# Value loads of a head in one shared 72-KB place, in 48-KB rows, and another order in the last head

## The chip, the cores and the metric

The kernel runs on one core of one Trainium2 chip. The metric is device time in microseconds (us) of one execution.

## The reference, cut to what matters

One token of a decoder layer: layer norm, attention over a long cache, a projection with residual, then a small two-layer network with residual.

```python
B, Sq, D = 1, 1, 640
H, Sk, Dh = 32, 32768, 192
q = (layernorm(x) @ wq).reshape(B, Sq, H, Dh).transpose(0, 2, 1, 3)
p = softmax(einsum("bhqd,bhkd->bhqk", q, k_cache) * Dh ** -0.5)
o = einsum("bhqk,bhkd->bhqd", p, v_cache)
h = x + o.transpose(0, 2, 1, 3).reshape(B, Sq, H * Dh) @ wo
out = h + relu(layernorm(h) @ w1) @ w2          # Dff = 1536
```

All inputs are bfloat16. The two caches hold 32 heads x 32768 rows x 192 numbers x 2 bytes each, 805 MB together; the weights bring the traffic to 825 MB. All of it is read once.

## The kernel before

A head's 32768 keys are handled in 8 chunks. In a chunk each of the 128 partitions has 32 rows. Of these DVE scores 12 or 16 (a multiply and a reduction) and PE the rest (transposes into PSUM, copies by ACT into SBUF, matmuls with the query). ACT takes the exponentials, and PE then multiplies them with the value rows, "the sums" below (`values`). SyncE issues all loads from one queue and waits, before each, until the place it writes is free; what is issued and not yet taken by the 16 DMA engines is what the texts call "the rings". GpSimd passes on the landing of a load to PE and DVE ("relay"; in the lines such a wait ends with `<-POOLq`).

```python
kt = [sbuf(f"kt{i}", [P, JK * Dh], bf16, 512) for i in range(NK)]   # 2 x 48 KB per partition
va = sbuf("va", [P, JK * Dh], bf16, 512)                            # 48 KB
vb = sbuf("vb", [P, JL * Dh], bf16, 512)                            # 24 KB

def vals(h, ld):
    if ld == 1:
        g.wait("PV", h, 1)                   # sums of chunk 1 of this head are done
    elif h > 0:
        g.wait("PV", h - 1, 3 if ld == 0 else NC - 1)
    src = rows(v_hd, h, P * JK * (ld // 2), JK)
    if ld < 2:
        src = src[:, ld * JL * Dh:(ld + 1) * JL * Dh]               # half a 48-KB row
    load((vb, vb, va)[ld][:], src, "dva" if ld == 2 else "dvb", "v", h, ld)
...
for h in range(LAST):
    keys(h, 0)
    vals(h, 0)
    keys(h, 1)
    for ld in ((2, 1) if h == 0 else (1, 2)):
        vals(h, ld)
```

So a head has five loads: keys 6.3 MB, values 3.1 MB, keys 6.3 MB, values 3.1 MB, values 6.3 MB. The last head is written by hand: its keys come in six loads, the last three small, then its values. PE's order there is (cut):

```python
def pe_end(g):
    ...
    transposes(g, h, 5);  scores_pe(g, h, 4)
    transposes(g, h, 6);  scores_pe(g, h, 5)
    transposes(g, h, 7);  scores_pe(g, h, 6)
    transposes(g, h, 8);  scores_pe(g, h, 7)
    transposes(g, h, 9)
    values(g, h, 2);      scores_pe(g, h, 8)
    values(g, h, 3);      scores_pe(g, h, 9)
    for c in (4, 5, 6, 7): values(g, h, c)
    values(g, h, 9); values(g, h, 8, 0); den_mm(g, h); values(g, h, 8, 1)
    ...                     # normalise, project, layer norm, the two layers with w1 and w2
```

The softmax here doesn't subtract the row's maximum and nothing guards it: scores larger than these inputs give would overflow.

Of the kernel before, what the change touches and what calls it, by code (L numbers as in the profile page):

```python
# [80 lines left out]
def kernel(  # L81
# [38 lines left out]

    full = [(c // 4, (c % 4) * J, J, JPS[c % 2]) + ((c // 2, (c % 2) * J) if c < 4 else (2, (c - 4) * J)) for c in range(NC)]

# [7 lines left out]
    def chunks(h):  # L130
        return ends if h == LAST else full

    NBM = max(JPS) * Dh // (2 * P)
# [17 lines left out]
    def sbuf(name, shape, dtype, align=32):  # L151
        return ctx.enter_context(nc.sbuf_tensor(name, shape, dtype, align_bytes=align))
# [5 lines left out]
    kt = [sbuf(f"kt{i}", [P, JK * Dh], bf16, 512) for i in range(NK)]  # L158
    va = sbuf("va", [P, JK * Dh], bf16, 512)
    vb = sbuf("vb", [P, JL * Dh], bf16, 512)  # L160
    wo_s = sbuf("wo_s", [P, 3, D], bf16, 512)
# [28 lines left out]
    for tag in ("ln1", "ln2"):  # L190
# [10 lines left out]

    wq_c = [kt[1][:, c * H * Dh:(c + 1) * H * Dh] for c in range(DT - 1)] + [va[:, 0:H * Dh]]
    assert (DT - 1) * H * Dh == JK * Dh and H * Dh <= JL * Dh

    k_at = {0: kt[0][:, 0:64 * Dh], 1: kt[0][:, 64 * Dh:128 * Dh], 2: kt[1][:, 0:64 * Dh],
            3: kt[1][:, 64 * Dh:104 * Dh], 4: kt[1][:, 104 * Dh:120 * Dh], 5: kt[1][:, 120 * Dh:128 * Dh]}
    v_at = {0: vb[:], 1: va[:, 0:JL * Dh], 2: va[:, JL * Dh:2 * JL * Dh],
            3: vb[:, 0:40 * Dh], 4: vb[:, 40 * Dh:56 * Dh], 5: vb[:, 56 * Dh:64 * Dh]}
    w1_s = kt[0][:, 0:DT * Dff].rearrange("p (c n) -> p c n", n=Dff)
# [7 lines left out]
    def v_tile(h, ld):  # L217
        return v_at[ld] if h == LAST else (vb, vb, va)[ld][:]

# [10 lines left out]
    def dma_program(g):  # L230
# [6 lines left out]
        def keys(h, ld):  # L237
            if h > 0:
                if ld == 0:
                    g.wait("PV", h - 1, 4 if h == 1 else 2)  # L240
                else:
                    g.wait("PV", h - 1, 5)
                g.wait("scs", h - 1, 4 * ld + 3)
            elif ld == 1:
                g.wait("att0")
            load(kt[ld][:], rows(k_hd, h, P * JK * ld, JK), f"dk{ld}", "k", h, ld)

        def vals(h, ld):

            if ld == 1:  # L250
                g.wait("PV", h, 1)
            elif h > 0:
                g.wait("PV", h - 1, 3 if ld == 0 else NC - 1)
            src = rows(v_hd, h, P * JK * (ld // 2), JK)
            if ld < 2:
                src = src[:, ld * JL * Dh:(ld + 1) * JL * Dh]
            load((vb, vb, va)[ld][:], src, "dva" if ld == 2 else "dvb", "v", h, ld)

        for c in range(DT):
            load(wq_c[c], wq_view[:, c * H * Dh:(c + 1) * H * Dh], f"dwq{c}", "wq", c)  # L260
        for h in range(LAST):
            keys(h, 0)
            vals(h, 0)
            keys(h, 1)
            for ld in ((2, 1) if h == 0 else (1, 2)):
                vals(h, ld)
            if h % 2 == 0 and h < LAST - 1:
                if h > 0:
                    g.wait("prj", h)
                load(wo_s[:], wo_view[h // 2], "dwo", "wo", h // 2)  # L270

        def end_keys(i, k0, jl, sem):
            load(k_at[i], rows(k_hd, LAST, k0, jl), sem, "k", LAST, i)
# [4 lines left out]

        g.wait("PV", LAST - 1, 2)
        g.wait("scs", LAST - 1, 3)  # L280
        end_keys(0, 0, JL, "dk0")
        g.wait("PV", LAST - 1, 3)
        end_values(0, 0, JL * Dh, "dvb", "v", LAST, 0)
        end_keys(1, P * JL, JL, "dke0")
        g.wait("PV", LAST - 1, 5)
        g.wait("scs", LAST - 1, NC - 1)
        end_keys(2, 2 * P * JL, JL, "dk1")
        k0 = P * JL * (NL - 1)
        at = []
# [4 lines left out]
        g.wait("PV", LAST - 1, NC - 1)  # L294
        end_values(1, 0, JL * Dh, "dva", "v", LAST, 1)

        for i in range(2):
# [17 lines left out]
    def pool_program(g):  # L315
        e = nc.gpsimd
        g.do(lambda: e.memset(wide[:], 0.0), "pool_act", ("ident0",))
        g.wait("ident0")
        g.do(lambda: e.affine_select(out=wide[:], in_=wide[:], compare_op=A.not_equal, fill=1.0, base=HE,
                                     pattern=[[-1, HE + P + 2 * (P - HE)]], channel_multiplier=1), "pool_row", ("ident",))  # L320
        def key(h, ld):
            relay(g, "k", h, ld)
            g.do(lambda: nc.gpsimd.sem_inc(sems["pool_dve"], 1))  # L323
            book_relay(g, "k", h, ld, sem="pool_dve")

        for h in range(LAST):
            key(h, 0)
            relay(g, "v", h, 0)
            key(h, 1)
            for ld in ((2, 1) if h == 0 else (1, 2)):  # L330
                relay(g, "v", h, ld)
            relay(g, "W", h)
        key(LAST, 0)
        relay(g, "v", LAST, 0)
        key(LAST, 1)
        key(LAST, 2)
        relay(g, "v", LAST, 1)
# [26 lines left out]
    def transposes(g, h, c):  # L364
        ld, off, jc, jp = chunks(h)[c][:4]
        src = k_tile(h, ld)
        if h == LAST and ld >= NL - 1:
            if c == 6 or ld >= NL:
                g.wait("k", h, ld)
        elif off == 0:  # L370
            g.wait("at", "k", h, ld)
# [43 lines left out]
    def values(g, h, c, part=None):  # L415
# [4 lines left out]
        if h == LAST and ld >= NL - 1:  # L420
            g.wait("vc", h, c)
        elif h == LAST and ld == 2:
            g.wait("vh", c - 4)
        elif off == 0:
            g.wait("at", "v", h, ld)
# [73 lines left out]

    SUMS = ((), (), (0,), (1,), (), (), (2, 3), (4,), (5, 6, 7))  # L500
    SUMS_0 = ((), (), (0,), (1,), (), (), (4,), (5,), (2, 3, 6, 7))

    def pe_head(g, h, turn=None):
        for c in range(NC + 1):
            if c == 0 and h > 0:
                den_mm(g, h - 1)
            if c < NC and c != 4:
                transposes(g, h, c)
            for d in (SUMS if h > 0 else SUMS_0)[c]:
                if c < NC:  # L510
                    values(g, h, d)
            if c > 0:
                scores_pe(g, h, c - 1)
            if c == 4:
                transposes(g, h, 4)
            if c == 2 and h > 0:
                o_turn(g, h - 1)
            if c == 4 and h > 0:
                project(g, h)
            if c == 6:  # L520
                q_spread(g, h + 1, turn)
        for d in (SUMS if h > 0 else SUMS_0)[NC]:
            values(g, h, d)

# [18 lines left out]
    def pe_end(g):  # L543
# [14 lines left out]
        transposes(g, h, 5)  # L558
        scores_pe(g, h, 4)
        transposes(g, h, 6)  # L560
        scores_pe(g, h, 5)
        transposes(g, h, 7)
# [3 lines left out]
        transposes(g, h, 9)  # L566
        values(g, h, 2)
        scores_pe(g, h, 8)
        values(g, h, 3)
        scores_pe(g, h, 9)  # L570
        values(g, h, 4)
        for c in (5, 6, 7):
# [72 lines left out]
    def act_head(g, h):  # L645
# [13 lines left out]

        behind = ((0,), (1,), (), (2,), (), (), (3,), (), (4,), ())  # L660
        for c in range(NCM):
# [7 lines left out]
        exp_pe(g, h, NCM - 1)  # L669
        for c in range(5, NCM):  # L670
            exp_dve(g, h, c)
# [242 lines left out]
```

## Time and profile before

| | kernel before |
|---|---|
| time, median | 1917.69 us (1916.72 to 1918.34, 3 runs) |
| span of the profiled run | 1915.3 us |
| last byte of the loads | 1911.3 us |
| end of the last sums on PE | 1904.5 us |
| DMA share and rate, 500 to 1500 us | 1.00, 433 to 434 GB/s |

The page's lines and the windows are shown in the prediction. The last byte and the end of the sums are read from the trace's records of DMA packets and matmuls. Two chains run into the end: the loads, whose last piece is w2, and PE, whose sums must be done before the projection and the two layers can follow. The end is the later of the two.

### The profile page before, as it was taken

To read this page: it belongs to the slowest core of one execution; us is meant where nothing else is said; L and a number is where in the kernel's file an instruction comes from. 1 tells how busy PE (TensorE), PEld (TensorE's weight loads), DVE (VectorE), ACT (ScalarE), POOL (GpSimd) and SP (SyncE) were. 2 spreads that over 40 slices of the span, in tenths; PEclk is the share of its full clock that TensorE was granted. 3 is DMA by queue.
4 is the path that set the end of the run, shared out by engine and by line. 5 is a ranking of instruction groups with operands and counts; after the bars stand their busy time and mean duration, and the time that the engine had idled before them with its cause. 6 is when DMAs were issued, how large, how long until landed. Compare 5 with 4: busy or idle time off the path is not lost.

```text
span 1915.3 us, 36109 instructions
## 1 busy us (share of the span) xinstructions
PE 1554.4 (81%) x15899; PEld 1089.8 (57%) x15899; DVE 1561.4 (82%) x731; ACT 939.4 (49%) x2000; POOL 1.0 (0%) x6
## 2 busy tenths in 40 slices
PE   7777787787888788878879887788788787878888
PEld 7455555554555555555556555556565555555565
DVE  2798787987878978789787888878798787987897
ACT  2455454554544544545545445545355454554454
POOL 0000000000000000000000000000000000000000
PEclk9888998888988889888898888898888898888988
DMA  9999999999999999999999999999999999999998
GB/s 409 428 436 428 430 438 430 437 435 431 436 431 432 435 433 429 437 430 437 435 431 433 434 434 434 432 429 437 430 436 434 430 437 431 435 430 437 431 433 369
DMA packets 29651, 825.29 MB, mean 431 GB/s; under 512 B 3132, under 2 KB 4669, under 8 KB 8125
## 3 DMA queue, kind: packets, MB, share of 16 engines
q1 hardware_dynamic: 29616, 824.98, 99.9%
q8 instruction: 15, 0.25, 0.0%
q14 instruction: 8, 0.06, 0.0%
q10 hardware_dynamic: 12, 0.00, 0.0%
HBM read 824.97 MB, written 0.00 MB: 431 GB/s over the span
## 4 chain that ended last, share of the span: by engine, by line
DVE 39%; DMA 39%; PE 15%; ACT 5%; issue 1%; DVEq 0%; SPq 0%; POOLq 0%
DMA kt<-in_A_k_cache_dram 35%; DVE sc L708 19%; DVE pr L705 18%; PE tp L381 7%; PE o_ps L362 7%; ACT kT L608 5%; DMA va<-in_A_v_cache_dram 2%; PE sp L362 1%; DVE o_pair L720 1%; DMA kt<-in_B_w_dram 1%; ACT pA L623 1%; DVE oT L730 0%; DMA kt<-in_A_wq_dram 0%; DVE rec L713 0%; DVE rec L714 0%
## 5 line engine op out<-in xcount | busy, mean ns | idle before, releaser
L705 DVE TENSOR_TENSOR pr<-kt,qb 128x2304 f32<-128x2304 bf16 (+2 forms) x257 | 756.7, 2944 | 313.8 <-POOLq L323 284.8
L608 ACT COPY kT<-tp 128x1024 bf16<-128x1024 bf16 (+1 forms) x898 | 814.3, 1017 | 271.4 <-PE tp L381 271.4
L381 PE MATMUL tp<-ident_f,kt 128*128 128x128 f32 x3456 | 592.0, 332 | 241.0 <-POOLq L344 165.2
L708 DVE TENSOR_REDUCE sc<-pr 128x12 f32<-128x2304 f32 (+2 forms) x257 | 756.1, 2942 | 8.9
L381 PEld LDWEIGHTS tp<-ident_f,kt 128*128 128x128 f32 x3456 | 487.0, 171 | 291.5 <-POOLq L344 170.9
L362 PE MATMUL o_ps<-va,pB 128*2 128x384 bf16 x1152 | 220.8, 340 | 59.8 <-POOLq L344 59.8
L362 PEld LDWEIGHTS sp<-qm,kT 128*128 128x128 bf16 x6912 | 197.6, 98 | 83.6 <-issue 42.8
L362 PE MATMUL sp<-qm,kT 128*128 128x2 bf16 x6912 | 214.6, 164 | 26.0 <-ACT pB L614 24.5
L362 PE MATMUL o_ps<-vb,pB 128*2 128x384 bf16 x1152 | 214.6, 332 | 22.6 <-ACT pA L623 22.0
L623 ACT ACTIVATE pA<-sc 128x12 bf16<-128x12 f32 (+2 forms) x257 | 58.3, 227 | 349.0 <-DVEq L65 349.0
L614 ACT ACTIVATE pB<-sp 128x20 bf16<-128x20 f32 (+2 forms) x258 | 52.4, 203 | 307.9 <-PE sp L362 307.9
L362 PEld LDWEIGHTS o_ps<-va,pB 128*2 128x2 bf16 x1152 | 94.1, 86 | 155.6 <-POOLq L344 67.5
L362 PE MATMUL o_ps<-va,pA 128*2 128x384 bf16 x896 | 171.5, 333 | 0.0
L362 PE MATMUL o_ps<-vb,pA 128*2 128x384 bf16 x896 | 166.7, 326 | 0.0
L362 PEld LDWEIGHTS o_ps<-vb,pB 128*2 128x2 bf16 x1152 | 90.3, 85 | 123.2 <-ACT pA L623 27.6
L362 PEld LDWEIGHTS o_ps<-va,pA 128*2 128x2 bf16 x896 | 77.0, 86 | 75.3 <-issue 8.3
L362 PEld LDWEIGHTS o_ps<-vb,pA 128*2 128x2 bf16 x896 | 75.2, 84 | 70.2
L614 ACT ACTIVATION_READ_ACCUMULATOR pB<-sp 128x1 f32 x258 | 55.1, 214 | 0.0
L623 ACT ACTIVATION_READ_ACCUMULATOR pA<-sc 128x1 f32 x257 | 53.1, 207 | 0.0
L362 PE MATMUL o_ps<-xn_ln,kt 128*96 128x1 bf16 (+1 forms) x316 | 22.3, 208 | 2.7 <-DMA kt<-in_A_wq_dram 2.7
L362 PEld LDWEIGHTS o_ps<-xn_ln,kt 128*96 128x96 bf16 (+1 forms) x316 | 22.1, 174 | 2.9 <-issue 2.8
L720 DVE TENSOR_SCALAR o_pair<-o_ps,rec 2x384 bf16<-2x384 f32 x32 | 19.3, 604 | 1.5 <-PE o_ps L362 0.4
(69 smaller groups left out, 187.3 us busy)
## 6 DMA issues: line engine op xcount, KB each, us to landing
kt<-in_A_k_cache_dram SPq DMA_DIRECT2D x62, 6144.0 KB, 26.7
vb<-in_A_v_cache_dram SPq DMA_DIRECT2D x63, 3072.0 KB, 19.0
va<-in_A_v_cache_dram SPq DMA_DIRECT2D x31, 6144.0 KB, 26.8
kt<-in_A_k_cache_dram SPq DMA_DIRECT2D x3, 3072.0 KB, 22.1
wo_s<-in_A_wo_dram SPq DMA_DIRECT2D x16, 480.0 KB, 19.0
kt<-in_A_wq_dram SPq DMA_DIRECT2D x4, 1536.0 KB, 10.9
va<-in_A_v_cache_dram SPq DMA_DIRECT2D x1, 3072.0 KB, 31.6
va<-in_A_v_cache_dram SPq DMA_DIRECT2D x2, 1536.0 KB, 36.4
```

The costliest lines, as they stand in the source:

```text
L362: return lambda: pe.matmul(o, lhsT=w, rhs=r, **kw)
L381: calls.append(lambda b=b, o=o: pe.transpose(out=dst[:, b, :], in_=src[:, o:o + 2 * P].bitcast(f32), identity=ident_f[:]))
L608: g.do(lambda: act.copy(out=kT[c % 2][:, b0:b0 + nb, :], in_=src[:, 0:nb, :].bitcast(bf16)), "act_pe", ("cp", h, c, k))
L614: g.do(lambda: act.activation(out=pB[c % NB][:, 0:jp], in_=sp[:, 0:jp], func=F.Exp, scale=SCALE, accum_out=dsums[:, 2 * c + 1:2 * c + 2]), ...
L623: g.do(lambda: act.activation(out=pA[c % NB][:, 0:jd], in_=sc[c % NC][:, 0:jd], func=F.Exp, scale=SCALE, accum_out=dsums[:, 2 * c:2 * c + ...
L705: g.chain(lambda: dve.tensor_tensor(out=pr[:, 0:j1 - j0, :], in0=src[:, (off + j0) * Dh:(off + j1) * Dh].rearrange("p (j d) -> p j d", d=D ...
L708: g.chain(lambda: dve.reduce_sum(out=sc[c % NC][:, j0:j1], in_=pr[:, 0:j1 - j0, :], axis=X), "dve")
L720: g.do(lambda: dve.tensor_scalar_mul(out=o_pair[:, :, 1, :], in0=o_ps[0:2, 0:2 * Dh].rearrange("q (i d) -> q i d", i=2), scalar1=rec[0:2, ...
```

## The change

Its intent: the values of a head come in two loads of 48-KB rows instead of three loads, two of which have 24-KB rows. The two share one 72-KB place: the first lies in thirds 0 and 1, the second in thirds 1 and 2. The chunks in the shared third are summed first. In the last head the second values are loaded ahead of the last keys, and PE and ACT take another order. The diff, cut to its core:

```diff
+    OFFS = (2, 3, 0, 1, 0, 1, 2, 3)
+    full = [(c // 4, OFFS[c] * J, J, JPS[c % 2], c // 4, OFFS[c] * J) for c in range(NC)]
...
-    va = sbuf("va", [P, JK * Dh], bf16, 512)
-    vb = sbuf("vb", [P, JL * Dh], bf16, 512)
+    va = sbuf("va", [P, (JK + JL) * Dh], bf16, 512)
...
         def vals(h, ld):
             if ld == 1:
                 g.wait("PV", h, 1)
             elif h > 0:
-                g.wait("PV", h - 1, 3 if ld == 0 else NC - 1)
+                g.wait("PV", h - 1, 5)
             ...                              # the old source and load go
+            load(v_tile(h, ld), rows(v_hd, h, P * JK * ld, JK), ("dva", "dvb")[ld], "v", h, ld)
...                                           # last head, loads
         end_keys(2, 2 * P * JL, JL, "dk1")
+        g.wait("PV", LAST - 1, 5)
+        end_values(1, 0, JL * Dh, "dvb", "v", LAST, 1)
         ...                                  # the three small key loads
         g.wait("PV", LAST - 1, NC - 1)
-        end_values(1, 0, JL * Dh, "dva", "v", LAST, 1)
...                                           # last head, PE
         scores_pe(g, h, 4)
+        scores_pe(g, h, 5)
+        values(g, h, 2)
+        values(g, h, 3)
         transposes(g, h, 6)
-        scores_pe(g, h, 5)
         transposes(g, h, 7)
         scores_pe(g, h, 6)
         transposes(g, h, 8)
         scores_pe(g, h, 7)
         transposes(g, h, 9)
-        values(g, h, 2)
         scores_pe(g, h, 8)
-        values(g, h, 3)
+        values(g, h, 4)
         scores_pe(g, h, 9)
-        values(g, h, 4)
```

In the loop, PE now takes the transposes and scores of four chunks and then their sums, in step with the loads.

More of the change, by code (lines that the diff above doesn't have):

```diff
@@ L117 @@
     assert Sk % (P * JK) == 0 and NK == 2 and NL == 4 and 2 * Dh == 3 * P and H % 2 == 0 and HE == 3 * P // 4 and DT == 5 and H >= 4
-    full = [(c // 4, (c % 4) * J, J, JPS[c % 2]) + ((c // 2, (c % 2) * J) if c < 4 else (2, (c - 4) * J)) for c in range(NC)]
+    OFFS = (2, 3, 0, 1, 0, 1, 2, 3)
+    full = [(c // 4, OFFS[c] * J, J, JPS[c % 2], c // 4, OFFS[c] * J) for c in range(NC)]
     ENDJ = (40, 16, 8)
@@ L131, in chunks, with leads @@
         return ends if h == LAST else full
+    def leads(h, c, i):
+        return c == 0 or chunks(h)[c - 1][i] != chunks(h)[c][i]
     NBM = max(JPS) * Dh // (2 * P)
@@ L199 @@
     mm = psum("mm", [P, 512])
-    wq_c = [kt[1][:, c * H * Dh:(c + 1) * H * Dh] for c in range(DT - 1)] + [va[:, 0:H * Dh]]
+    wq_c = [kt[1][:, c * H * Dh:(c + 1) * H * Dh] for c in range(DT - 1)] + [va[:, JK * Dh:JK * Dh + H * Dh]]
     assert (DT - 1) * H * Dh == JK * Dh and H * Dh <= JL * Dh
@@ L206 @@
             3: kt[1][:, 64 * Dh:104 * Dh], 4: kt[1][:, 104 * Dh:120 * Dh], 5: kt[1][:, 120 * Dh:128 * Dh]}
-    v_at = {0: vb[:], 1: va[:, 0:JL * Dh], 2: va[:, JL * Dh:2 * JL * Dh],
-            3: vb[:, 0:40 * Dh], 4: vb[:, 40 * Dh:56 * Dh], 5: vb[:, 56 * Dh:64 * Dh]}
+    v_at = {0: va[:, 0:JL * Dh], 1: va[:, JL * Dh:2 * JL * Dh], 2: va[:, 2 * JL * Dh:3 * JL * Dh],
+            3: va[:, 0:40 * Dh], 4: va[:, 40 * Dh:56 * Dh], 5: va[:, 56 * Dh:64 * Dh]}
     w1_s = kt[0][:, 0:DT * Dff].rearrange("p (c n) -> p c n", n=Dff)
@@ L217, in v_tile @@
     def v_tile(h, ld):
-        return v_at[ld] if h == LAST else (vb, vb, va)[ld][:]
+        return v_at[ld] if h == LAST else va[:, ld * JL * Dh:(ld * JL + JK) * Dh]
     names = ["pool_pe", "act_pe", "dve_pe", "act_dve", "dve_act", "dve", "dve_row", "pe_dve", "pool_row", "pool_dve", "pool_act", "pe_act", "pe", "dve_sp", "act_row"]
@@ L238, in keys @@
             if h > 0:
-                if ld == 0:
-                    g.wait("PV", h - 1, 4 if h == 1 else 2)
-                else:
-                    g.wait("PV", h - 1, 5)
+                g.wait("PV", h - 1, 4 * ld)
                 g.wait("scs", h - 1, 4 * ld + 3)
@@ L252, in vals @@
             elif h > 0:
-                g.wait("PV", h - 1, 3 if ld == 0 else NC - 1)
-            src = rows(v_hd, h, P * JK * (ld // 2), JK)
-            if ld < 2:
-                src = src[:, ld * JL * Dh:(ld + 1) * JL * Dh]
-            load((vb, vb, va)[ld][:], src, "dva" if ld == 2 else "dvb", "v", h, ld)
+                g.wait("PV", h - 1, 5)
+            load(v_tile(h, ld), rows(v_hd, h, P * JK * ld, JK), ("dva", "dvb")[ld], "v", h, ld)
         for c in range(DT):
@@ L261, in dma_program @@
         for h in range(LAST):
-            keys(h, 0)
-            vals(h, 0)
-            keys(h, 1)
-            for ld in ((2, 1) if h == 0 else (1, 2)):
+            for ld in range(NK):
+                keys(h, ld)
                 vals(h, ld)
@@ L276, in end_values @@
             load(v_at[ld][:, c0:c1], rows(v_hd, LAST, P * JL * ld, JL)[:, c0:c1], sem, *label)
-        g.wait("PV", LAST - 1, 2)
+        g.wait("PV", LAST - 1, 0)
         g.wait("scs", LAST - 1, 3)
@@ L282, in dma_program @@
         g.wait("PV", LAST - 1, 3)
-        end_values(0, 0, JL * Dh, "dvb", "v", LAST, 0)
+        end_values(0, 0, JL * Dh, "dva", "v", LAST, 0)
         end_keys(1, P * JL, JL, "dke0")
-        g.wait("PV", LAST - 1, 5)
+        g.wait("PV", LAST - 1, 4)
         g.wait("scs", LAST - 1, NC - 1)
         end_keys(2, 2 * P * JL, JL, "dk1")
+        g.wait("PV", LAST - 1, 5)
+        end_values(1, 0, JL * Dh, "dvb", "v", LAST, 1)
         k0 = P * JL * (NL - 1)
@@ L326, in pool_program @@
         for h in range(LAST):
-            key(h, 0)
-            relay(g, "v", h, 0)
-            key(h, 1)
-            for ld in ((2, 1) if h == 0 else (1, 2)):
+            for ld in range(NK):
+                key(h, ld)
                 relay(g, "v", h, ld)
@@ L369, in transposes @@
                 g.wait("k", h, ld)
-        elif off == 0:
+        elif leads(h, c, 0):
             g.wait("at", "k", h, ld)
@@ L423, in values @@
             g.wait("vh", c - 4)
-        elif off == 0:
+        elif leads(h, c, 4):
             g.wait("at", "v", h, ld)
@@ L496, in q_spread @@
         pe_group(g, calls, ("qs", h), "pe_act")
-    SUMS = ((), (), (0,), (1,), (), (), (2, 3), (4,), (5, 6, 7))
-    SUMS_0 = ((), (), (0,), (1,), (), (), (4,), (5,), (2, 3, 6, 7))
     def pe_head(g, h, turn=None):
-        for c in range(NC + 1):
-            if c == 0 and h > 0:
-                den_mm(g, h - 1)
-            if c < NC and c != 4:
-                transposes(g, h, c)
-            for d in (SUMS if h > 0 else SUMS_0)[c]:
-                if c < NC:
-                    values(g, h, d)
-            if c > 0:
-                scores_pe(g, h, c - 1)
-            if c == 4:
-                transposes(g, h, 4)
-            if c == 2 and h > 0:
-                o_turn(g, h - 1)
-            if c == 4 and h > 0:
+        if h > 0:
+            den_mm(g, h - 1)
+        for ld in range(NK):
+            c0 = 4 * ld
+            transposes(g, h, c0)
+            transposes(g, h, c0 + 1)
+            scores_pe(g, h, c0)
+            transposes(g, h, c0 + 2)
+            scores_pe(g, h, c0 + 1)
+            if ld == 0 and h > 0:
+                o_turn(g, h - 1)
+            transposes(g, h, c0 + 3)
+            scores_pe(g, h, c0 + 2)
+            values(g, h, c0)
+            scores_pe(g, h, c0 + 3)
+            if ld == 1:
+                q_spread(g, h + 1, turn)
+            for d in (1, 2, 3):
+                values(g, h, c0 + d)
+            if ld == 0 and h > 0:
                 project(g, h)
-            if c == 6:
-                q_spread(g, h + 1, turn)
-        for d in (SUMS if h > 0 else SUMS_0)[NC]:
-            values(g, h, d)
     def pe_norm(g):
@@ L658, in act_head @@
             return
-        behind = ((0,), (1,), (), (2,), (), (), (3,), (), (4,), ())
+        behind = ((0,), (1,), (), (2,), (), (3,), (4,), (), (5,), ())
         for c in range(NCM):
@@ L669, in act_head @@
         exp_pe(g, h, NCM - 1)
-        for c in range(5, NCM):
+        for c in range(6, NCM):
             exp_dve(g, h, c)
```

## The prediction

> **What bounds the kernel now.** I read the page's busy shares first, then the DMA lines, then long stretches of the span, then the waits and the end in order of time. In the page's busy line, the two slices and the queue line, no compute engine is full, while the DMA engines are busy in every slice:
>
> ```profile
> PE 1554.4 (81%) x15899; PEld 1089.8 (57%) x15899; DVE 1561.4 (82%) x731; ACT 939.4 (49%) x2000; POOL 1.0 (0%) x6
> ...
> DMA  9999999999999999999999999999999999999998
> ...
> DMA packets 29651, 825.29 MB, mean 431 GB/s; under 512 B 3132, under 2 KB 4669, under 8 KB 8125
> ...
> q1 hardware_dynamic: 29616, 824.98, 99.9%
> ```
>
> Packets in flight take 99.9% of what 16 engines have over the whole span. The stretches (columns: length, busy time and count of each engine, granted PE clock, DMA share, GB/s) say that the share is 1.00 and the rate 433 to 434 GB/s from beginning to end, and falls only in the last 10 us:
>
> ```profile
> 500.00:1000.00 500.00, 405.26 (x4110) 280.98 (x4109) 411.75 (x191) 248.30 (x528) 0.00 (x0) 0.89 1.00 433
> 1000.00:1500.00 500.00, 411.76 (x4128) 290.19 (x4127) 415.99 (x185) 248.52 (x530) 0.00 (x0) 0.86 1.00 434
> ...
> 1905.00:1915.30 10.30, 5.66 (x146) 4.75 (x146) 1.59 (x12) 0.82 (x3) 0.00 (x0) 0.71 0.50 184
> ```
>
> I also counted, from the trace's DMA packets, how many were in flight at each instant: summed over the time from first packet (1.98 us after the start) to last (1911.3 us), the capacity with fewer than 16 in flight is only 2.6 us, and about 1.4 us of that is in the last 3 us. So there are no bubbles in the middle for a better load order to close. The chain of waits names key loads, DVE and PE in turn (DVE 39%, DMA 39%), because each load is issued when its place is freed; that is a loop with slack in it, not three bounds. DVE itself waits for keys to land, 284.8 us in 31 waits:
>
> ```profile
> DVE pr L705 <- POOLq L323: 284.8, 31, 31.8
> ```
>
> The slack of the issues is in the sync engine's timeline:
>
> ```profile
> 737.17 0.33 SPq L232 DMA_DIRECT2D kt<-in_A_k_cache_dram  x1
> 758.80 0.33 SPq L232 DMA_DIRECT2D vb<-in_A_v_cache_dram  x1
> 759.17 0.43 SPq L232 DMA_DIRECT2D va<-in_A_v_cache_dram  x1
> ```
>
> The key load issued at 737.17 lands near 764, so the value load behind it is in the queue about 5 us before the rings would run dry.
>
> **What the Trainium skill says.** "DMA: Bandwidth & Descriptors", section "Where 436 GB/s comes from", puts the fabric ceiling at 16 ports x 32 B x 850 MHz = 435.2 GB/s. The trace agrees: 433 to 434 GB/s over 500 us. The same page, "Why small descriptors are slow (HBM only)", gives a fixed cost of about 3 cycles per packet and 32 B of metadata. The trace shows a fixed cost: by size, its packets take 912 ns for 24 KB and 1815 ns for 48 KB, so two of 24 KB cost 1824 ns, 9 ns more than one of 48 KB; a 4-byte completion packet takes 9 ns as well. The same page, "Latency and other measured facts", gives about 600 ns to first byte on this path; here the first issue is at 0.96 us and the first packet at 1.98, 1.0 us, which I use. "TensorE: Matmul & The Clock Gate", section "Part 1: The HAM clock gate (the "warmup" mystery)", says that an idle window of about 3.4 us halves the PE clock until a similar time of work. The trace shows the halving even after a shorter wait, 2.83 us (granted clock 0.58 in 728 to 732 us), where ten value matmuls took 3.15 us, against 1.79 us warm:
>
> ```profile
> 728.05 3.15 PE L362 MATMUL o_ps<-va,pB 128*2 128x384 bf16 x10 [2.83 <-POOLq L344]
> ...
> 738.60 1.14 PE L362 MATMUL o_ps<-va,pA 128*2 128x384 bf16 x6
> ```
>
> **The change, part by part.**
>
> *Loads.* A head now has four loads (keys, values, keys, values) of 128 rows of 48 KB, instead of five of which two are of 24-KB rows. The bytes are the same. Per head and engine, 16 packets of 24 KB (16 x 912 = 14592 ns) become 8 of 48 KB (8 x 1815 = 14520 ns), and one completion packet of 9 ns goes: 81 ns. This is on the path, because the engines are never free: 31 heads x 0.081 = 2.5 us off the time at which the last byte arrives. The packets should fall by 31 x (128 + 16) = 4464, from 29651 to 25187.
>
> *Buffers.* The first value load of a head lies in thirds 0 and 1, the second in 1 and 2; the chunks in the shared middle third are summed first. So the second load waits for the sums of chunks 0 and 1, and the next head's first for those of chunks 4 and 5. Is each issued in time? Let T be when a value load lands. The key load behind it takes 8 x 1.815 = 14.5 us, so the next value load must be issued by about T + 13. At T, PE should already have the transposes and the first three score groups of these keys (the keys landed at T - 14.5; transposes took about 0.125 us each, 54 of them 6.8 us, but copies by ACT, 14 x 1.02 = 14.3 us, and the DVE scores of the first two chunks, 5.1 + 6.7 us, pace them). From T: relay 0.5, sums of a chunk 3.0 us warm or 4.5 cold, scores 0.75 to 0.9 (1.5 cold), in the second half of a head 0.8 of query matmuls, sums 3.0. That is T + 8 to T + 10.5. Slack 2.5 to 5 us. Next head's first keys wait for the DVE scores of four chunks: T - 14.5 + 0.5 + 24.7 = T + 11, needed by T + 27.5. Its second keys are freed at about T + 39 and needed 17 us later. All in time, so the load stream should stay unbroken. Median issue to landing should become about 32 us for keys (three loads deep) and 20 us for values.
>
> *PE and DVE order.* Both process the same instructions; PE has sums in two bursts per head instead of split. PE's 20.5 us and DVE's 24 us of each half head lie beside 29 us of loads, so this costs nothing unless it delays an issue.
>
> *Last head.* Its second values move ahead of its last keys (7.3 us of load), so its last keys land 7.3 us nearer to the end, and PE does two sums before, not after, the last transposes. The end before:
>
> ```profile
> 1903.64 0.81 PE L362 MATMUL o_ps<-vb,pA 128*2 128x384 bf16 x4
> ...
> 1909.31 0.94 PE L362 MATMUL attT<-h1T,kt 128*128 128x1 bf16 x30 [0.45 <-ACT h1T L678]
> ...
> 1911.31 0.69 PE L362 MATMUL attT<-h1T,kt 128*128 128x1 bf16 x15 [0.29 <-DMA kt<-in_B_w_dram]
> ```
>
> The last matmuls wait for the last weights. Had they been there, the 60 matmuls from 1909.31 would have ended after about 2.0 us (0.94 for 30, twice 0.5 for 15), at 1911.2, not 1912.0. So the compute chain is only 0.8 us behind the loads: of the 2.5 us, only 0.8 can be gained unless this chain gets earlier too. Does it? Counted from the last byte, in the new order DVE ends its last scores about 11 us before it, as now (the last head's keys then wait for DVE, not DVE for them). PE: I estimate scores of chunk 5 done near 1878, two sums until 1884, the last 30 transposes with ten ACT copies (about 9.5 us with the activations between) until 1893, then five sums and the tail, 11 to 12 us, to 1904.6 to 1906, against 1904.4 now. So the end moves between -0.8 and +1.5 us. Sum: 1917.7 - 0.8 to 1917.7 + 1.5; I also allow that PE's new order wins a little more than I see, and take -0.9, i.e. **1916.8 us**.
>
> **Rivals.**
> 1. *The value loads are issued late.* If PE is cold and ACT is held up by DVE (it does exponentials and copies in one order), the second value load comes at T + 14 or later and the rings run dry in each half of a head. 1 us late is 62 us in all, 3.2%: 1980 us. For it: the halved clock after 2.83 us of waiting. Against: 2.5 us of slack even with the cold clock. This is the main risk of a clear loss.
> 2. *Bytes arrive faster in long rows.* If 48-KB rows had a better rate than 9 ns per packet, all would gain. Against: 24576 B / 912 ns = 26.95 and 49152 / 1815 = 27.08 B/ns, 0.5% apart, on half of the value traffic at most: the 2.5 us above and no more.
> 3. *The tail turns from loads to compute.* As worked out: the gain of the stream does not show at the end, time 1916.9 to 1919.2. I half believe it.
> 4. *Deeper queues remove bubbles.* Only 2.6 us of capacity was unused and most of that at the ends, so below 1 us.
>
> **Range and chances.** Without rivals 1 and 3, 1917.7 - 2.5 = 1915.2; with the tail bound, up to 1919. Runs of before spread by 1.6 us. A small leak of issues (0.05 us per value load) adds 3 us. Range 1914.2 to 1920.5. Faster by 2% would need 1879.3 us, below the 1895.7 us that 825 MB take at 435.2 GB/s: 1%. Slower by 2% needs 0.6 us lost on every value load: 6%. Within 2%: 93%.
>
> **What would show it.** DMA share 1.00 and 433 to 435 GB/s in the 500-us stretches, packets 25187, key landing near 32 us. Rival 1 would show as a share under 0.98 there, with sync waits for sums ending at T + 13 or later and fewer than 16 packets in flight once per half head. The tail: the last weight matmuls no longer wait for the DMA but follow their predecessors, with the end of the last sums at 1904 to 1906. I am wrong if the share drops, if the engine time of a 48-KB packet in the new place is not 1815 ns, or if the end of the last sums moves by over 3 us.

## The result

The changed kernel took 1920.04 us (median of 4 runs, 1919.76 to 1921.25), the kernel before 1917.22 us in 4 runs (1916.72 to 1918.34). The ratio is 1.0015, with a 95% interval of 0.9998 to 1.0032: the same, within 2%. (Ratios here are the mean time of one kernel's runs over that of the other's of the same rounds, so not quite the ratio of the medians quoted.) The point, 1916.8, was 3.2 us too low. By the medians the change cost 2.8 us. The interval just includes 1; but the four runs lie above every execution of the kernel before on record, the highest of which took 1919.17 us. Small as the loss is, it is worth following, because two parts of the change pull in opposite directions.

The profile after, by the same views: busy time and load queue on the page, then two stretches of the span (length, busy time and count of PE, weight loads, DVE, ACT, GpSimd, granted clock as a share of PE's full clock, DMA share, GB/s).

```profile
PE 1577.7 (82%) x15899; PEld 995.2 (52%) x15899; DVE 1561.4 (81%) x731; ACT 937.6 (49%) x2000; POOL 1.0 (0%) x6
...
DMA packets 25185, 825.28 MB, mean 430 GB/s; under 512 B 2635, under 2 KB 4172, under 8 KB 7628
...
q1 hardware_dynamic: 25152, 824.98, 99.6%
```

```profile
500.00:1000.00 500.00, 412.62 (x4124) 257.17 (x4122) 415.08 (x191) 247.78 (x528) 0.00 (x0) 0.92 1.00 434
1000.00:1500.00 500.00, 411.79 (x4125) 256.11 (x4124) 415.15 (x185) 248.09 (x530) 0.00 (x0) 0.92 1.00 434
...
1905.00:1918.00 13.00, 8.43 (x165) 6.01 (x163) 2.44 (x14) 0.82 (x3) 0.00 (x0) 0.76 0.22 81
```

The packets fell to 25185 (25187 predicted; on the load queue by exactly the 4464), and the stream is as whole as before: share 1.00, 434 GB/s. The load queue's share of the whole span fell from 99.9% to 99.6%, and the last stretch has a share of only 0.22: the loads are done earlier. Their last byte came at 1909.1 us instead of 1911.3. Yet the span grew from 1915.3 to 1918.0 us. From the last byte to the end it was 4.0 us before and 8.9 us after. So the loop gained 2.2 us, and the end lost more.

The timeline of PE at the end of the changed kernel (start, time, instruction, count, idle time before and what ended it):

```profile
1877.34 0.90 PE L354 MATMUL sp<-qm,kT 128*128 128x2 bf16 x30 [0.22 <-ACT pB L604]
1880.25 0.75 PE L354 MATMUL sp<-qm,kT 128*128 128x2 bf16 x24 [2.01 <-ACT pB L604]
1880.93 3.36 PE L354 MATMUL o_ps<-va,pB 128*2 128x384 bf16 x10
...
1887.88 2.41 PE L373 MATMUL tp<-ident_f,kt 128*128 128x128 f32 x17
...
1893.46 0.60 PE L354 MATMUL sp<-qm,kT 128*128 128x2 bf16 x18 [0.93 <-ACT pB L604]
...
1895.44 3.03 PE L354 MATMUL o_ps<-va,pB 128*2 128x384 bf16 x10
...
1907.32 0.81 PE L354 MATMUL o_ps<-va,pA 128*2 128x384 bf16 x4
...
1912.97 1.76 PE L354 MATMUL attT<-h1T,kt 128*128 128x1 bf16 x60 [0.36 <-ACT h1T L668]
```

PE waits 2.01 us for an exponential. ACT in the same stretch shows why it comes so late, behind three copies of the next chunk:

```profile
1877.10 2.91 ACT L598 COPY kT<-tp 128x1024 bf16<-128x1024 bf16 x3
1879.81 0.30 ACT L604 ACTIVATE pB<-sp 128x20 bf16<-128x20 f32 x1
```

Then PE sums at half speed (ten value matmuls in 3.36 us; "warm" ones, with the full clock granted, take 1.79), and only at 1887.88 begins the last transposes. The last sums end at 1908.1, 3.7 us later than the 1904.5 of before. The 60 matmuls with w2 run in one piece after the activation before them. They no longer wait for the DMA: the end is now set by PE.

In the kernel before, the same transposes lay earlier, before the values of chunk 2 had come:

```profile
1877.07 1.38 PE L381 MATMUL tp<-ident_f,kt 128*128 128x128 f32 x9
...
1884.44 1.52 PE L381 MATMUL tp<-ident_f,kt 128*128 128x128 f32 x6
...
1885.89 3.21 PE L362 MATMUL o_ps<-va,pB 128*2 128x384 bf16 x10
```

PE did the last transposes between 1877 and 1886 there, while those values were on their way: they landed at 1885.6, and the sums followed at once.

The landings of the loop came out as foreseen. DVE's waits for keys, which the prediction did not speak of, are now twice as many and half as long each, in sum nearly the same:

```profile
DVE pr L695 <- POOLq L317: 293.9, 62, 31.6
...
kt<-in_A_k_cache_dram SPq DMA_DIRECT2D x62, 6144.0 KB, 33.4
va<-in_A_v_cache_dram SPq DMA_DIRECT2D x62, 6144.0 KB, 21.0
```

The first of these lines is from the waits (sum, times, longest), the others from the DMA issues (count, size, median us from issue to landing). Keys land 33.4 us after their issue, values 21.0; 32 and 20 had been predicted.

### The profile page after: what moved, and what is told of

The parts are those of the page before. It is cut to its first block, busy times and chain, and to the rows that moved or that the text cites. A ratio compares the mean times of both kernels' runs of the same rounds, so it can differ in the third digit from the quotient of the medians.

```text
span 1918.0 us, 35954 instructions
## 1 busy us (share of the span) xinstructions
PE 1577.7 (82%) x15899; PEld 995.2 (52%) x15899; DVE 1561.4 (81%) x731; ACT 937.6 (49%) x2000; POOL 1.0 (0%) x6
## 2 busy tenths in 40 slices
DMA packets 25185, 825.28 MB, mean 430 GB/s; under 512 B 2635, under 2 KB 4172, under 8 KB 7628
## 3 DMA queue, kind: packets, MB, share of 16 engines
q1 hardware_dynamic: 25152, 824.98, 99.6%
## 4 chain that ended last, share of the span: by engine, by line
DMA 57%; DVE 37%; PE 3%; issue 1%; ACT 1%; DVEq 0%; SPq 0%; POOLq 0%
DMA kt<-in_A_k_cache_dram 51%; DVE pr L695 18%; DVE sc L698 18%; DMA va<-in_A_v_cache_dram 6%; PE o_ps L354 3%; ACT kT L598 1%; PE sp L354 0%; DVEq L65 0%; SPq L235 0%; PE attT L354 0%; PE mm L354 0%; DVE o_pair L710 0%; PE tp L373 0%; ACT pB L604 0%; POOLq L317 0%
## 5 line engine op out<-in xcount | busy, mean ns | idle before, releaser
L354 PE MATMUL o_ps<-va,pB 128*2 128x384 bf16 x2304 | 501.2, 371 | 186.7 <-POOLq L336 147.9
L373 PE MATMUL tp<-ident_f,kt 128*128 128x128 f32 x3456 | 514.8, 286 | 121.5 <-ACT kT L598 77.1
L373 PEld LDWEIGHTS tp<-ident_f,kt 128*128 128x128 f32 x3456 | 375.5, 143 | 222.9 <-ACT kT L598 171.3
L354 PEld LDWEIGHTS o_ps<-va,pB 128*2 128x2 bf16 x2304 | 198.8, 92 | 410.6 <-POOLq L336 153.4
L354 PE MATMUL o_ps<-va,pA 128*2 128x384 bf16 x1792 | 371.2, 352 | 0.0
L354 PEld LDWEIGHTS o_ps<-va,pA 128*2 128x2 bf16 x1792 | 161.9, 90 | 172.9 <-issue 53.7
L604 ACT ACTIVATE pB<-sp 128x20 bf16<-128x20 f32 (+2 forms) x258 | 61.5, 238 | 109.8 <-PE sp L354 109.8
L354 PEld LDWEIGHTS attT<-oT,wo_s 128*128 128x128 bf16 x465 | 13.6, 96 | 10.3 <-issue 9.9
L354 PE MATMUL attT<-oT,wo_s 128*128 128x1 bf16 x465 | 16.3, 164 | 0.3 <-DVE oT L720 0.3
L354 PEld LDWEIGHTS mm<-dsums,ones_mat 128*128 128x128 f32 x64 | 9.5, 188 | 10.6 <-issue 10.6
## 6 DMA issues: line engine op xcount, KB each, us to landing
kt<-in_A_k_cache_dram SPq DMA_DIRECT2D x62, 6144.0 KB, 33.4
```

Of the source, the lines that this page charges most:

```text
L354: return lambda: pe.matmul(o, lhsT=w, rhs=r, **kw)
L373: calls.append(lambda b=b, o=o: pe.transpose(out=dst[:, b, :], in_=src[:, o:o + 2 * P].bitcast(f32), identity=ident_f[:]))
L604: g.do(lambda: act.activation(out=pB[c % NB][:, 0:jp], in_=sp[:, 0:jp], func=F.Exp, scale=SCALE, accum_out=dsums[:, 2 * c + 1:2 * c + 2]), ...
```

## The experiments

Theory A: the loss is made in the last head, on PE. From the scores of chunk 5 on PE has no rest until the end, and the last transposes, at ACT's copying pace, have no sums beside them. Theory B: only PE's new order is to blame. Theory C: the shared place in the loop loses the time.

| run | median us (range) | ratio to before (95%) | last byte | end of last sums |
|---|---|---|---|---|
| before (its first 4 runs) | 1917.22 (1916.72 to 1918.34) | | 1911.3 | 1904.5 |
| changed | 1920.04 (1919.76 to 1921.25) | 1.0015 (0.9998 to 1.0032) | 1909.1 | 1908.1 |
| e1_old_order | 1917.98 (1916.98 to 1918.83) | 1.0001 (0.9987 to 1.0014) | 1909.4 | 1907.1 |
| e2_old_last_head | 1917.31 (1915.32 to 1918.26) | 0.9996 (0.9983 to 1.001) | 1909.3 | 1906.4 |
| e3_only_last_head | 1921.36 (1919.57 to 1921.81) | 1.0018 (1.0005 to 1.0032) | 1911.2 | 1908.5 |
| e4_interleaved | 1915.31 (1914.87 to 1915.79) | 0.9989 (0.9975 to 1.0002) | 1909.2 | 1903.1 |
| e5_split_rows | 1918.3 (1917.51 to 1918.44) | 1.0002 (0.9989 to 1.0016) | 1911.8 | 1905.6 |
| e6_late_value_loads | 2038.86 (2036.35 to 2040.58) | 1.0634 (1.0618 to 1.065) | 2030.6 | |
| e7_old_loop_interleaved | 1917.36 (1916.66 to 1918.2) | 0.9996 (0.9983 to 1.001) | 1912.5 | 1904.7 |
| e8_one_swap | 1917.62 (1916.71 to 1918.19) | 0.9998 (0.9984 to 1.0012) | 1909.2 | 1906.1 |
| e9_one_sum_later | 1963.47 (1959.39 to 1972.87) | 1.0243 (1.0225 to 1.026) | 1967.2 | |

In every call the kernel before ran nine times beside these; its medians there were 1917.38, 1917.7 and 1917.12 us. So runs of different calls (e4 against e5, e7 or e8, and any against the changed kernel) can differ by some 0.6 us for the call alone. The last two columns are of the profiled run, on its own clock, and each comes from one execution: the slowest of its runs in e1, e2, e7 and e9, the fastest in the changed kernel, e5 and e6. All results were correct.

### e1_old_order: the loads of the change, the last head's order of before

```diff
         scores_pe(g, h, 4)
-        scores_pe(g, h, 5)
-        values(g, h, 2)
-        values(g, h, 3)
         transposes(g, h, 6)
+        scores_pe(g, h, 5)
...                        # and so on as in the kernel before; ACT's order of exponentials too
```

> The changed kernel, but PE and ACT process the last head in the order of the kernel before (all transposes ahead of the sums of chunks 2 to 4); the loads stay as changed. Theory A (the loss of 2.8 us is made in the last head on PE, which from the scores of chunk 5 on has no rest until the end, with the last transposes at ACT's copying pace and no sums beside them): with the last keys landing at 1881 the transposes now wait for them, end near 1890, and all sums follow: sums end at 1907 to 1909 as in the changed kernel (1908.0), time 1919 to 1921. Theory B (only PE's new order is to blame): sums end at 1904 to 1905, time 1916 to 1917. Theory C (the loop's shared place loses the time): 1920, with the last byte arriving later than 1909.

```profile
1881.39 2.18 PE L373 MATMUL tp<-ident_f,kt 128*128 128x128 f32 x9 [2.58 <-DMA kt<-in_A_k_cache_dram]
...
1889.83 1.94 PE L354 MATMUL o_ps<-va,pB 128*2 128x384 bf16 x10
```

In PE's timeline the transposes of chunk 6 wait 2.58 us for the last keys, which the load order of the change puts behind the second values, and the sums of chunk 2 begin at 1889.83, where the kernel before had begun them at 1885.89. The sums end at 1907.1, within A's 1907 to 1909, and not at B's 1904 to 1905; but this is the slowest of the five executions. The median, 1917.98, fell between A's and B's figures, and two of the five (1916.98, 1917.18) lie in B's range or next to it. So e1 does not decide between A and B. By the medians the old order takes back most of the 2.8 us (ratio to the kernel before 1.0001), so most of the loss goes with PE's and ACT's new order; but the 2.2 us of the loop still don't show: with the keys late, the old order waits for them.

### e2_old_last_head: the changed loop, the whole last head as before

```diff
-        g.wait("PV", LAST - 1, 5)
-        end_values(1, 0, JL * Dh, "dvb", "v", LAST, 1)
...                        # the three small key loads
         g.wait("PV", LAST - 1, NC - 1)
+        end_values(1, 0, JL * Dh, "dvb", "v", LAST, 1)
...                        # and PE's and ACT's order of the kernel before
```

> The changed loop with the whole last head of the kernel before (load order and PE and ACT order). Theory A: last byte at 1909 as in the changed kernel; DVE starts the last head about 1.5 us later than before, because the last whole keys land after DVE has run dry, so the sums end near 1905.9 and the time is 1917.5 to 1918.5, i.e. two thirds of the loss gone. Theory B: 1916 to 1917. Theory C: 1920 still.

The time, 1917.31 us, is that of before (ratio 0.9996), 0.2 us under A's range. The last byte came at 1909.3, so C falls: the loop gains its 2 us here too. But the sums end at 1906.4 (in the slowest of the five executions), 1.9 us later than before, so PE eats the gain. Part of it was foreseen. DVE starts the last head 1.5 us later (1850.65 against 1849.11), because in the changed loop a head's second keys come only after DVE has run dry. DVE's timeline around the second keys of head 30 (counting from 0), first before, then after the change:

```profile
1824.03 2.56 DVE L705 TENSOR_TENSOR pr<-kt,qb 128x2304 f32<-128x2304 bf16 x1 [0.25 <-DVE sc L708]
```

```profile
1825.50 2.56 DVE L695 TENSOR_TENSOR pr<-kt,qb 128x2304 f32<-128x2304 bf16 x1 [3.19 <-POOLq L317]
```

Before, DVE came straight from the first keys' work; after, it waited 3.19 us for the second keys. On PE, 1.1 of the 1.9 us are already there at the scores of chunk 4 (1877.41 against 1876.31), and 0.9 come from slower sums of chunk 2 (3.36 + 1.86 against 3.21 + 1.14 us). That DVE's 1.5 us became PE's 1.1 is argued, not tested.

### e3_only_last_head: the loop of before, only the last head changed

```diff
+        g.wait("PV", LAST - 1, NC - 1)
+        end_values(1, 0, JL * Dh, "dva", "v", LAST, 1)
...                        # the three small key loads
-        g.wait("PV", LAST - 1, NC - 1)
-        end_values(1, 0, JL * Dh, "dva", "v", LAST, 1)
...                        # and PE's and ACT's order of the change
```

> The loop of the kernel before (three value places, 24-KB rows) with only the last head changed: its second values ahead of its last keys, and the new PE and ACT order. Theory A: last byte at 1911.3 as before, DVE as before, sums end at 1906 to 1907 instead of 1904.4, time 1918 to 1919, slower than before by 1 to 1.5 us. Theory C: as before, 1917.2.

It took 1921.36 us, 4.0 us over the kernel before (1917.38), and the interval, 1.0005 to 1.0032, is clear of 1. The last byte came at 1911.2, as before. The last head alone makes the loss, in the old loop as in the new one; C falls again. My size was too small: I had given the sums 1906 to 1907, and they ended at 1908.5. I had credited them with DVE's earlier start, but in this order they don't wait for DVE:

```profile
1879.31 0.80 PE L362 MATMUL sp<-qm,kT 128*128 128x2 bf16 x24 [2.01 <-ACT pB L614]
1880.04 3.36 PE L362 MATMUL o_ps<-va,pB 128*2 128x384 bf16 x10
...
1887.82 2.41 PE L381 MATMUL tp<-ident_f,kt 128*128 128x128 f32 x17
```

The same 2.01 us of waiting, the same cold sums, and the last transposes at the same 1887.8 as in the changed kernel.

### e4_interleaved: the changed kernel with sums between the last transposes

```diff
         scores_pe(g, h, 4)
-        scores_pe(g, h, 5)
         values(g, h, 2)
-        values(g, h, 3)
+        scores_pe(g, h, 5)
         transposes(g, h, 6)
+        values(g, h, 3)
         transposes(g, h, 7)
         scores_pe(g, h, 6)
         transposes(g, h, 8)
+        values(g, h, 4)
         scores_pe(g, h, 7)
         transposes(g, h, 9)
         scores_pe(g, h, 8)
-        values(g, h, 4)
+        values(g, h, 5)
         scores_pe(g, h, 9)
-        for c in (5, 6, 7):
+        for c in (6, 7):
```

> The changed kernel with another PE order of the last head: each group of the last transposes is followed by the sums of one chunk, so that ACT copies while PE sums, and the sums of chunk 2 take the place where PE waited 2.0 us for an exponential. Loads untouched. Theory A: sums end at 1902 to 1904.5, the end is again set by the last weights (last byte at 1909.1 plus 4.0), time 1914.8 to 1916.5, 3.5 to 5 us under the changed kernel and 1 to 2.4 us under the one before. Theory C: no gain against the changed kernel, 1919 to 1920.

```profile
1878.35 1.79 PE L354 MATMUL o_ps<-va,pB 128*2 128x384 bf16 x10
...
1881.66 1.18 PE L373 MATMUL tp<-ident_f,kt 128*128 128x128 f32 x9
1882.77 1.46 PE L354 MATMUL o_ps<-va,pB 128*2 128x384 bf16 x8
...
1901.96 0.40 PE L354 MATMUL mm<-dsums,ones_mat 128*128 128x20 f32 x2 [0.59 <-ACT pA L614]
1902.29 0.81 PE L354 MATMUL o_ps<-va,pA 128*2 128x384 bf16 x4
...
1908.23 1.92 PE L354 MATMUL attT<-h1T,kt 128*128 128x1 bf16 x60 [0.36 <-ACT h1T L669]
```

The sums of chunk 2 start at 1878.35 without the wait, and ACT copies while PE sums. Near the end PE waits for ACT's exponentials of DVE's scores (0.59 us before the row sums of the softmax), which means that PE is no longer behind DVE. The sums end at 1903.1, 5.0 us earlier than in the changed kernel. By PE's timeline the clock is 2.8 of these: from their start to that of the next group, the sums of chunk 2 took 4.26 us in the changed kernel and 2.69 here, those of chunk 4 took 3.93 and 2.69. The time is 1915.31 us: all five runs lie below all nine of the kernel before (1916.17 at the lowest). The interval of the ratio, 0.9975 to 1.0002, still touches 1, so 2.1 us is the difference of the medians, not a gain beyond doubt. The loads and PE now end within about a microsecond of each other: last byte at 1909.2, last matmul with w2 at 1910.2. The two are nearly level: the 60 matmuls run on but for some 0.13 us before the last 15, whose part of w2 landed at 1909.4 while they were running. This version has the lowest median, and the loads of the change are untouched in it.

### e7_old_loop_interleaved: the loop of before under the same good end

The edit is that of e3 with the order of e4.

> The loop of the kernel before (24-KB rows, three value places) with the changed last head's loads and the interleaved PE order. Compute then ends well before the last byte, so the last byte sets the end: 1911.2 plus 4.0 is a span of 1915.2 to 1915.6, time 1917 to 1918, and the difference to the interleaved kernel with the changed loop (1915.3) is what the loop's longer rows are worth, 2 to 2.5 us. If instead the changed loop gave nothing, both would have the same time.

```profile
1912.45 0.70 PE L362 MATMUL attT<-h1T,kt 128*128 128x1 bf16 x15 [0.33 <-DMA kt<-in_B_w_dram]
```

With this order in the old loop, PE waits for w2 again, and the time is 1917.36 us, as expected. Against e4 (1915.31) the changed loop is worth 2.05 us, or 1.7 when each is taken against the kernel before, once the end lets it through; all five runs of e4 lie below all five of e7. The order alone gives the old kernel nothing, since it was bound by the last byte already. In this profiled run the last byte was 1.2 us later than in the two other runs of the old loop; the trace has 107 packets that took over 2% longer than the median of their size, against 48 in the kernel before and 46 in e3.

### e8_one_swap: one exchange on PE

```diff
         scores_pe(g, h, 4)
-        scores_pe(g, h, 5)
         values(g, h, 2)
+        scores_pe(g, h, 5)
         values(g, h, 3)
```

> The changed kernel with one swap in PE's order of the last head: the sums of chunk 2 go ahead of the scores of chunk 5, into the 2.0 us in which PE waited for an exponential. If that wait and the halved clock after it (sums of chunk 2 in 4.3 instead of 2.8 us) are one part of the loss and the last transposes without sums beside them the other: the sums end 2.0 to 3.5 us earlier, 1904.6 to 1906, time 1916.5 to 1918. If the wait only moves to a later place: under 1 us.

```profile
1878.25 3.26 PE L354 MATMUL o_ps<-va,pB 128*2 128x384 bf16 x10
```

The wait of 2.0 us is gone, and the sums end at 1906.1, 2.0 us earlier; the time falls by 2.4 us (medians) to 1917.62. That part was right, at the slow edge of the range. But I had put the halved clock down to that wait, and it is there without it: ten matmuls in 3.26 us at 1878.25, where e4 had 1.79 us at 1878.35 after the very same instructions. In these runs the halving at this place is not settled by the wait before it. In all traces the granted clock changes only after multiples of 3.41 us; e8's record is at half from 1878.39 to 1881.80, e4's is full from 1863.38 to 1904.34, and e7, with e4's order, is at half from 1880.60. So of the other 3.0 us up to e4's 1903.1, 1.7 are the clock at this place (1878.25 to 1883.37 in e8 for the sums of chunk 2 and the scores after them, 1878.35 to 1881.79 in e4), which may be chance, and 1.3 come with the sums between the last transposes. These also seem to keep the clock up: the first ten sums of chunk 4 took 1.79 us in all three traces that have them (e4, e5, e7), 2.59 to 3.36 in the three that have none there (changed, e3, e8). No run tests that by itself.

### e5_split_rows: the interleaved kernel in 24-KB rows

```diff
-            load(v_tile(h, ld), rows(v_hd, h, P * JK * ld, JK), ("dva", "dvb")[ld], "v", h, ld)
+            src = rows(v_hd, h, P * JK * ld, JK)
+            for n in range(2):
+                load(v_tile(h, ld)[:, n * JL * Dh:(n + 1) * JL * Dh], src[:, n * JL * Dh:(n + 1) * JL * Dh], ...)
```

> The interleaved kernel, with each value load of the loop issued as two loads of 24-KB rows, one straight after the other, into the same place under the same waits. This measures the row length alone. If a packet has a fixed cost of 9 ns, every value load costs each engine 16 x 912 instead of 8 x 1815 ns and one more completion packet, 81 ns; 62 loads: last byte 5.0 us later (near 1914.2), packets 25152 + 62 x 144 = 34080 on the load queue, time 1919 to 1921. Rival (the row length is worth nothing and the earlier last byte came from elsewhere): last byte stays at 1909, time 1915.3.

```profile
DMA packets 34114, 825.29 MB, mean 431 GB/s; under 512 B 3627, under 2 KB 5164, under 8 KB 8620
```

The packets are as many as foreseen (34080 on the load queue), but the last byte came 2.7 us later (1911.8 against 1909.2), not 5.0, and the time is 1918.3, below the expected range. The records say where the other half went. Summed over 16 engines, the packets took 4.85 us more (1914.56 against 1909.71 us), as 9 ns each would make it. But the overlap, the time with more than 16 packets in flight, grew by 2.25 us: a packet starts while the end of its predecessor still runs. So a packet costs about 2.66 us / (62 x 9) = 4.8 ns of stream, not 9, by one execution of each kernel; that of e5 was its fastest, 0.8 us under its median, so the cost may be somewhat higher.

### e6_late_value_loads and e9_one_sum_later: how close the issue is to the edge

```diff
             if ld == 1:
-                g.wait("PV", h, 1)
+                g.wait("PV", h, 3)           # e9: 2
             elif h > 0:
-                g.wait("PV", h - 1, 5)
+                g.wait("PV", h - 1, 7)       # e9: 6
```

> The interleaved kernel, with each value load waiting for all four sums of the load before (PV 3 and PV 7) instead of the first two, as it would have to if the two loads shared one 48-KB place without a free third. Theory (only the issue in time keeps the stream whole): in the changed kernel's trace the sums of chunk 3 end about 14.5 us after a first value load is taken up, those of chunk 7 about 13 us after a second; with 1.0 us to the first packet that is 0.5 to 2 us too late each, 31 x 2.4 = 75 us in all (50 to 110), time 1965 to 2025, DMA share near 0.96. Rival (the queue has so much in it that the issue does not matter): 1915.3.

> The interleaved kernel, with each value load waiting for one sum more than in the change (PV 2 and PV 6). It places the edge: in the changed kernel's trace those sums end about 11.1 us and 10.6 us after the value load is taken up, with 1.0 us to the first packet that is 12.3 us at most, and the key load in front ends about 14 us after. If the slack is what the trace says, nothing changes: DMA share 1.00, last byte near 1909.2, time 1914.5 to 1916. If the rings need more than 1.7 us of lead, the share falls to 0.98 or 0.99 and the time rises by 10 us and more.

e6 took 2038.86 us, over the expected range. The DMA share in a stretch of 500 us fell to 0.96:

```profile
500.00:1000.00 500.00, 384.99 (x3821) 242.25 (x3818) 385.11 (x176) 232.74 (x494) 0.00 (x0) 0.87 0.96 403
```

By the records of packets, capacity without a packet in flight came to 78.9 us, against 2.5 us in e4; the 75 us of my estimate were that part. Another 44.7 us are packets that took longer: 1299 of the 48-KB packets took more than 2% over the 1815 ns, 2369 ns on the mean. With the packets placed in order on 16 engines, some 780 of them are the first after a gap of over 0.1 us (an estimate: the records don't name the engine).

e9 was to show that one sum later is harmless, and it was not: 1963.47 us. The edge is nearer than I had worked out. I had counted from the landing of a value load to the end of the key load behind it, 14.5 us. But the 16 engines don't finish a load together. In the changed kernel's trace the first engine is done with a load 2.7 us (median) before the last; 1.9 us in the kernel before. A load has landed when the last engine is done; the first engine to run dry does so 2.7 us earlier than my count. Measured from the end of the instruction that issues a value load to the moment at which the first engine finishes the load in front, the lead is 3.5 us in the changed kernel (median; 1.85 at the least), 0.9 us in e9 and -0.4 us in e6. The first packet comes 1.0 us after the start of such an instruction, but 0.63 us after its end (0.96, 1.35 and 1.98 us at the first load). So the changed loop has some 2.9 us of slack in the median and 1.2 us at worst; the kernel before had a median lead of 10.1 us and 2.7 at the least.

The busy share of the DMA engines hardly shows the loss in e9, the rate does:

```profile
500.00:1000.00 500.00, 406.51 (x4024) 255.25 (x4025) 406.31 (x182) 241.29 (x522) 0.00 (x0) 0.89 1.00 425
```

Of the 58 us by which its last byte is later than e4's, 37 are packets that took longer (and count as busy), and 21 are unused capacity; this is the slowest of its five executions.

## Why the prediction was right or wrong

**Range and class** held: 1920.04 us lies in 1914.2 to 1920.5, near its top, and the change is the same within 2%. For the range that was partly luck. The case that came, the tail bound by compute, had been given 1919.2 at most, and the room above came from a leak of late issues that did not come. The point had the wrong direction: 0.9 us faster was forecast, 2.8 slower was measured.

**Loads** were right. The last byte came 2.2 us earlier (2.5 predicted), the load queue's packets are exact, and e7 against e4 gives the loop 1.7 to 2.05 us. The working behind the 2.5 us was half right: by e5 about half of the 9 ns per packet is overlapped, so longer rows alone explain about 31 x 9 x 4.8 ns = 1.3 us (an estimate). The rest goes with packets that were slower than usual in the kernel before: its packets took 3.3 us less in sum after the change, where 9 ns each explains 2.5. Why they were slower was not tested.

**Buffers**: issue in time was right (value loads were issued 7.5 to 9.1 us after T, median 8.2, near the early end of T + 8 to T + 10.5). "Slack 2.5 to 5 us" was too much: it was 2.9 in the median and 1.2 at the least. Its term "must be issued by about T + 13" left out that the first engine runs dry 2.7 us before the last. Rival 1 did not come, but e9 shows that one sum later it does.

**Last head**: this is the step that failed. "PE: I estimate scores of chunk 5 done near 1878, two sums until 1884, the last 30 transposes [...] until 1893" and the end at 1904.6 to 1906. Measured: scores at 1881.0, two sums until 1887.9, transposes and their scores until 1895.5, end at 1908.1. By the prediction's own sign ("if the end of the last sums moves by over 3 us") this part was wrong: it moved by 3.7 us. Two things were missing from its terms. The scores of chunk 5 wait for the exponential of chunk 4, which ACT does only after the copies of chunk 5 (2.0 us, recovered in e8). The sums of chunk 2 ran at half clock, 3.36 instead of 1.79 us for their first ten matmuls (3.21 in the kernel before), and those of chunk 4 again (3.03; 1.79 before). About 1.0 us was there already at the scores of chunk 4 (1877.34 against 1876.31). The last transposes took less than allowed, 7.6 us instead of 9. So the chain that had 0.8 us to spare moved by 3.7 us: 3.7 - 0.8 = 2.9 us, and 2.8 was measured.

The prediction's own sum has two slips here: 1893 plus 11 to 12 us is 1904 to 1905; and sums that end 0.2 to 1.6 us later, with 0.8 us to spare, move the end by -0.6 to +0.8 us, not by -0.8 to +1.5. So its 1919.2 was already too wide for what it had worked out, and the miss is larger than it looks.

**Rival 3**, the end turning from loads to compute, is what happened, beyond the 1919.2 us that I gave it. I half believed it and put the point on the other half. e3 shows that the last head alone costs 4.0 us, e4 that another order on PE removes the cost with the loads as they are. **Rivals 2 and 4** did not show: the rate in the middle was 433 to 434 GB/s before and 434 after, and unused capacity 2.6 us in both.

## What to carry to other kernels

In a kernel that is bound by its loads, a gain in the stream reaches the time only as far as the compute after the last byte allows; work out how far behind the second chain is, in the last stage by itself, before counting the gain. In such a last stage, lay work that waits for nobody (here sums) between the steps that go back and forth between two engines (here transposes and copies). In e4 PE's order alone ended the chain 5.0 us earlier without touching a load; 2.0 of these are a wait taken away (e8), and by PE's timeline over half go with the clock, part of which may be chance. And when buffers are shared more tightly, count the lead of an issue up to the first DMA engine that runs dry, not to the landing of the load.

## What the Trainium skill lacked or had wrong

- "DMA: Bandwidth & Descriptors" says that the engines of a load finish independently, but gives no time for it: in the changed kernel the first of 16 was done 2.7 us (median) before the last of a 6.3-MB load, 1.9 us in the kernel before. This decides how early the next load must be issued.
- The same page has nothing on packets after the rings ran dry: in e6, 1299 packets of 48 KB took 2369 ns on the mean instead of 1815, 44.7 us in all, on top of 78.9 us of gaps.
- Its fixed cost per packet, described for small descriptors, shows in the records at 24 and 48 KB too, 9 ns per packet; but successive packets overlap, and e5 gives some 4.8 ns of stream for each.
- Its 600 ns to first byte does not say from where it counts. Here the first packet came 1.0 us after the start of the issuing instruction and 0.63 us after its end, also in e6 at five issues into idle engines (0.62 to 0.64); from the end the two agree.
- "TensorE: Matmul & The Clock Gate" speaks of an idle window of about 3.4 us. Here the clock was halved after waits of 2.0 and 2.8 us, and in e8 at a place without a wait (ten value matmuls in 3.26 us), while e4 ran the same instructions there in 1.79 us. The page does say that the window runs free and that this varies from run to run; e4 and e8 agree with that, and so do the traces, whose clock changes only after multiples of 3.41 us.
